# An S5 scan and a long convolution on one core: the written order of the steps replaced by another one

## The chip, the cores and the metric

The kernel runs on one core of a Trainium2 chip. The metric is the device time of one execution in microseconds (us). Traces are of one profiled execution each. Engines are called PE (TensorE), DVE (VectorE), ACT (ScalarE), POOL (GpSimd) and SP (SyncE, which here issues DMAs); PEld is PE's loading of weights.

## The reference

Two layers on sequences of 2048 steps and 640 channels, whose outputs are laid side by side. A is a diagonal complex state space model (640 states) with input and output projections; B multiplies a gated long convolution by q.

```python
def _A_ref(x, Lambda_re, Lambda_im, B_re, B_im, C_re, C_im, log_dt, Dskip):
    Lam_bar = jnp.exp(dt * Lam)
    B_bar = ((Lam_bar - 1.0) / Lam)[:, None] * Bmat
    Bu = jnp.einsum("bld,pd->blp", x + 0j, B_bar)
    for t in range(L):
        h = Lam_bar[None, :] * h + Bu[:, t, :]
    y = 2.0 * jnp.einsum("blp,dp->bld", hseq, Cmat).real + x * Dskip[None, None, :]

def _B_ref(q, k, v, shift_k, ssm_k, ssm_D):
    for t in range(ks):
        k_shift = k_shift + k_pad[:, t:t + S, :] * shift_k[:, ks - 1 - t][None, None, :]
    kv = k_shift * v
    ...
    y = y + kv * ssm_D[None, None, :]
    return q * y

return jnp.concatenate([a, b], axis=-1)
```

The line left out is a convolution of kv with ssm_k along the sequence, by FFT of length 4096.

## The kernel before

The work is cut into named items. `make_plan` gives each item an engine, the items that it needs and a function that records its instructions; `ORDER`, one long string, lists all items in the order in which they are recorded. Each engine carries out its own instructions strictly in that order, and SP likewise starts its DMAs in that order: an instruction that waits holds up everything behind it on its engine. Semaphores between engines follow from the data. The deps, costs and latencies in the plan don't act at run time; only `ORDER` does.

A name with `@0`, `@2`, `@4` or `@6` writes to one of four PSUM slots (`ps0` to `ps3`, two banks each). A slot can be written again when what was in it has been copied out. A name with `!` takes the item's other engine: an eviction (a copy from PSUM to SBUF) goes to DVE rather than ACT (`copy`, lines 467 and 469), and the swap of k's halves, `kS`, to ACT rather than DVE (`swap_k`, lines 625 and 627).

Layer A has five groups of 128 states, `j` = 0 to 4, and four sequence phases `s` (step mod 4). `v{s}_{j}` are the input matmuls (L522, L524, L525), `ve` their evictions; phase 0 is rotated (`rs`), scanned (`sc`, L551), turned back (`ra`, `rout`), and the other phases follow from it by `oa{s}_{j}` (L563 to L565) and `od{s}_{j}` (L570, L571), all on DVE. `p{i}_{s}` is the output projection for 128 rows of a phase (L584, with the skip term at L589): it needs all five groups of its phase. `yo` evicts it, `yd` stores it. The projection (3, 2) is done in two halves, `a` and `b`.

Layer B has five groups `G` of 128 channels. `kT`, `vT`, `hs`, `qi` load (the first two with a DMA transpose), `tap` is the short convolution on PE (L650), `kv` the product with v on DVE (L655), `kvo` and `kvs` store kv and load it back rearranged. Two matmul stages of a transform follow: `s1` (L666) and `s2` (L679), each with four parts for the filter (`h`) and for kv (`k`), each evicted (`s1he`, `s1ke`, `s2he`, `s2ke`). The product in frequency is `ya` (L691, L692) and `y` (L697) on DVE, in two halves. `inv` (L705 to L708) is four parts of the inverse, evicted by `zs`; `zt` transposes the result by DMA (L716); `fin` is the last matmul stage (L724), `ob` the product with q on DVE (L729), `od_G` the store. `y{G}_0` is needed by `inv{G}_0` and `inv{G}_1`, `y{G}_1` by the other two.

The first lines of `ORDER` prepare constants, tables and the first input matmuls. After them, items of layer A and layer B alternate.

Of the kernel before, what the change touches and what calls it, by code (L numbers as in the profile page):

```python
# [940 lines left out]

ORDER = """
lv1! pc lsk lv0! lv4 B0 pc2 dc dc3 wm0@0 lv2 zer lv3 pc3 dc2 wm1@2 B1 gp1 dsel x1 tsk@4 gp0 bt0@6 tske@4 dS0 tv@0 wm2@2 pp tve@0
bt1@4 x2 pk den exp wm3@2 be1@4 rho Fi wm4@0 rr be0!@6 v1_1@2 tp0 dD trig1 prr drhs G1 lam tp1 v1_0@4 x3 dL1 pow ve1_1@2 dL2 dL0
tab0 dcm@0 gam v2_1@6 gp3 aRM vT0 ve1_0!@4 tab1 tp2 dcol@0 dG B3 v2_0@2 G3 kT0 tp3 ve2_1!@6 tab2 dRM v3_1@4 ve2_0!@2 tab3 tp4 B4
x0 v3_0@0 tab4 ve3_1!@4 hp0 kS0 G0 hp1 bg1@6 ve3_0!@0 B2 H0 bg2@2 gp2 CT0 bge1!@6 tap0_0@4 H1 tap0_1@0 hp2 kv0_0@4 v0_0@6
kv0_1@0 bge2@2 hp3 H2 dS1 hs0 kvo0 bg3@4 H3 ve0_0!@6 kT1 v0_1@2 rs0 bge3@4 ca0 sc0 bg0@0 ve0_1@2 v1_3@6 bge0@0 rs1 G2 v1_2@4 sc1
ve1_3@6 CT1 v2_3@2 ve1_2@4 ra1 kS1! kvs0 had0 rout1 s1h0_2@0 vT1 nH ve2_3@2 s1h0_3@6 v2_2@4 oa2_1 s1he0_2@0 od2_1 s1he0_3@6
oa3_1 s1h0_0@2 od3_1 ve2_2@4 tap1_0@0 s1he0_0@2 s1h0_1@6 cs0 v3_2@4 s1he0_1@6 ra0 ca1 rout0 tap1_1@2 ve3_2@4 hs1 oa2_0 s1k0_1@6
v0_2@4 s1ke0_1@6 od2_0 kT2 kv1_0@0 kv1_1@2 s1k0_2@6 ve0_2@4 s1k0_3@0 cs1 s1k0_0@2 s1ke0_3@0 v3_3@4 s1ke0_0@2 qi0 kvo1 rs2  # L950
s1ke0_2@6 s2k0_3@0 dS2 ve3_3@4 s2h0_3@2 sc2 s2k0_1@6 s2ke0_3@0 v0_3@4 s2he0_3@2 s2ke0_1@6 had1 ra2 kS2! rout2 s2k0_2@0 vT2 oa2_2
v1_4@2 ve0_3@4 od2_2 s2ke0_2@0 kvs1 rs3 s2h0_1@6 ve1_4@2 s2h0_0@4 s2h0_2@0 s2he0_1@6 v2_4@2 s2he0_0@4 sc3 s2he0_2@0 ra3 s1h1_1@6
ve2_4@2 s1h1_0@4 tap2_1@0 rout3 s1he1_1@6 tap2_0@2 kv2_1@0 s1he1_0@4 s1h1_2@6 kT3 kv2_0@2 s1he1_2@6 s2k0_0@0 s1h1_3@4 s2ke0_0@0
s1k1_2@6 ya0_1 v3_4@2 s1ke1_2@6 kvo2 hs2 s1he1_3@4 dS3 y0_1 s2h1_3@0 ve3_4@2 s1k1_0@6 s1k1_3@4 ya0_0 s2he1_3@0 v0_4@2 kS3! y0_0
s1ke1_3@4 vT3 inv0_2@0 ve0_4!@2 s1ke1_0@6 inv0_1@4 rs4 zs0_2@0 s2h1_1@2 zs0_1@4 tap3_0@6 s2he1_1@2 s1k1_1@0 had2 sc4 inv0_0@4
kvs2 s1ke1_1@0 s2h1_0@2 zs0_0@4 inv0_3@0 kv3_0@6 s2he1_0@2 tap3_1@4 zs0_3@0 ra4 s2k1_2@2 kT4 s2k1_3@6 s2ke1_2@2 kv3_1@4 s2k1_0@0
s2ke1_3@6 s2h1_2@2 rout4 s1h2_1@4 s2ke1_0@0 kvo3 s2k1_1@6 oa2_3 zt0_0 s1he2_1@4 p0_0@0 od2_3 s2ke1_1@6 oa2_4 s2he1_2@2 od2_4
kS4! s1h2_3@4 s1k2_2@6 p1_0@2 oa1_1 od1_1 zt0_1 yo0_0@0 s1ke2_2@6 dS4 s1he2_3@4 ya1_1 s1k2_1@0 s1h2_0@6 yo1_0@2 yd0_0 p0_2@4 vT4
s1ke2_1@0 s1he2_0@6 y1_1 ya1_0 s1h2_2@2 yd1_0 yo0_2@4 s1k2_0@0 hs3 s1k2_3@6 s1he2_2@2 p1_2@4 s1ke2_0@0 kvs3 y1_0 s1ke2_3@6 yd0_2
oa1_3 s2h2_1@2 od1_3 yo1_2@4 s2h2_2@0 s2he2_1@2 yd1_2 fin0_1@6 oa1_0 inv1_0@4 s2he2_2@0 od1_0 s2h2_0@2 zs1_0@4 fin0_0@0  # L960
s2he2_0@2 inv1_1@4 ob0_1@6 inv1_2@2 zs1_1@4 oa3_2 inv1_3@6 zs1_2@2 ob0_0@0 s2k2_0@4 zs1_3@6 od3_2 s2k2_1@2 od_0 s2k2_3@0
s2ke2_0@4 zt1_0 s2k2_2@6 oa1_4 s2ke2_1@2 tap4_1@4 od1_4 s2ke2_2@6 s1k3_3@2 s1ke3_3@2 s2h2_3@6 kv4_1@4 s2ke2_3@0 s1k3_2@2 ya2_0
s1k3_0@4 s2he2_3@6 zt1_1 p2_2@0 s1ke3_2@2 s1ke3_0@4 had3 y2_0 qi1 s1h3_1@6 ya2_1 yo2_2@0 s1h3_0@2 tap4_0@4 s1he3_1@6 yd2_2
s1h3_2@0 s1he3_0@2 s1k3_1@6 kv4_0@4 s1ke3_1@6 inv2_0@2 s1he3_2@0 y2_1 fin1_0@6 kvo4 s1h3_3@4 zs2_0@2 inv2_1@0 hs4 oa3_3
s1he3_3@4 inv2_2@2 od3_3 zs2_1@0 s2h3_3@4 zs2_2@2 oa3_4 s2h3_1@0 s2he3_1@0 ob1_0@6 fin1_1@2 s2he3_3@4 s2k3_0@0 ob1_1@2 kvs4
inv2_3@6 s2ke3_0@0 od3_4 s2k3_1@4 zs2_3@6 od_1 s2k3_3@2 s2h3_0@0 s2ke3_1@4 oa1_2 zt2_0 p3_0@6 s2he3_0@0 od1_2 s2ke3_3@2 had4
ya3_0 s2h3_2@4 yo3_0@6 s2k3_2@0 s2he3_2@4 s1h4_0@2 s2ke3_2!@0 s1h4_3@6 s1he4_0@2 s1h4_2@4 y3_0 s1h4_1@0 s1he4_2@4 p2_0@2
s1he4_3@6 zt2_1 ya3_1 s1he4_1@0 s1k4_0@4 y3_1 yo2_0@2 s1k4_3@6 s2h4_0@0 s1ke4_0@4 s1k4_2@2 oa3_0 yd2_0 s1ke4_3@6 inv3_3@4 yd3_0
qi2 od3_0 s2he4_0@0 inv3_2@6 s1ke4_2@2 inv3_0@0 zs3_2!@6 zs3_3@4 inv3_1@2 zs3_0!@0 fin2_0@6 zs3_1@2 s1k4_1@4 s2h4_3@0 s1ke4_1@4
zt3_0 s2h4_2@2 s2he4_3!@0 s2he4_2@2 s2k4_3@4 s2k4_2@0 s2ke4_3@4 ob2_0@6 fin2_1@2 s2ke4_2@0 s2k4_0@4 zt3_1 ob2_1@2 s2k4_1@6  # L970
s2ke4_0@4 s2h4_1@0 ya4_1 p0_3@2 s2ke4_1@6 od_2 s2he4_1@0 y4_1 p0_1@4 yo0_3@2 ya4_0 yd0_3 y4_0 fin3_0@6 yo0_1@4 inv4_2@0 yd0_1
inv4_0@2 qi3 zs4_2@0 inv4_3@4 zs4_0@2 inv4_1@0 zs4_3@4 fin3_1@2 zs4_1!@0 p3_3@4 zt4_1 ob3_1@2 p2_3@0 zt4_0 ob3_0@6 p1_3@2 od_3
p1_1@6 yo1_3@2 yd1_3 p2_1@2 yo1_1@6 qi4 yd1_1 p3_1@6 yo2_1@2 yd2_1 yo2_3@0 yd2_3 fin4_1@2 yo3_1@6 fin4_0@0 ob4_1@2 yd3_1 p3_2a@6
p3_2b@2 yo3_3@4 ob4_0@0 yd3_3 od_4 yo3_2a@6 yo3_2b@2 yd3_2a yd3_2b
"""


# [66 lines left out]
```

## Time and profile before

| what | value |
|---|---|
| median of 3 runs | 201.82 us (201.66 to 201.91) |
| the profiled execution, whole time | 201.48 us |
| its span, first to last instruction | 199.7 us |
| PE busy | 185.5 us, 93% of the span |
| PEld busy | 128.0 us, 64% |
| DVE busy | 165.0 us, 83% |
| ACT busy | 153.9 us, 77% |
| POOL busy | 24.8 us, 12% |
| DMA | 32.61 MB, 163 GB/s in the mean |
| granted TensorE clock | 0.998 |

Busy time of an engine counts its instructions from start to end, once where they overlap. A PE instruction that waits in the middle of a group can look busy. The span leaves out what lies around the kernel's own instructions, 1.8 us here. Lines are those of the kernel printed above.

### The profile page before, as it was taken

The page shows a single profiled execution, that of the slowest core. Times are in us where ns is not written, and L with a number is a line of the kernel's source. Part 1 is how long each engine was busy: PE and PEld are TensorE (multiplying, and loading weights), DVE is VectorE, ACT ScalarE, POOL GpSimd, SP SyncE. Part 2 cuts the span into 40 slices and gives each one's busy share as a digit, 9 for nine tenths or more (in the row PEclk, how much of TensorE's full clock was granted, in tenths as well). Part 3 has the DMA queues.
Part 4 walks back from the last instruction along what each step waited for, and adds up shares of the span by engine and source line. Part 5 has one row for each costly group of instructions (what it writes and reads, how often), then busy time and mean ns, then how long its engine had stood idle before and what let it go on. Part 6 is the DMA issues. An engine that isn't in the chain of part 4 may idle for free. (4 is left out here: it accounts for less than half of the span.)

```text
span 199.7 us, 7507 instructions
## 1 busy us (share of the span) xinstructions
PE 185.5 (93%) x3328; PEld 128.0 (64%) x3340; DVE 165.0 (83%) x285; ACT 153.9 (77%) x190; POOL 24.8 (12%) x55
## 2 busy tenths in 40 slices
...
GB/s 129 201 216 220 207 235 221 187 207 110 82 159 186 147 67 27 241 163 83 213 193 176 154 173 132 155 256 136 203 151 147 147 170 150 129 153 198 147 126 138
DMA packets 125052, 32.61 MB, mean 163 GB/s; under 512 B 120919, under 2 KB 124380, under 8 KB 125020
## 3 DMA queue, kind: packets, MB, share of 16 engines
...
q10 hardware_dynamic: 40, 0.01, 0.0%
...
## 5 line engine op out<-in xcount | busy, mean ns | idle before, releaser
L522 PE MATMUL ps<-xT,BT 128*128 128x512 bf16 x188 | 47.6, 379 | 1.2 <-DMA xT<-in_A_x_dram 0.6
L584 PE MATMUL ps<-Cs,hs 128*128 128x320 bf16 x240 | 36.3, 299 | 0.3 <-ACT Xs L469 0.3
L469 ACT CAST BT<-ps 128x640 bf16<-128x640 f32 (+3 forms) x20 | 14.0, 703 | 25.1 <-PE ps L589 24.4
L522 PEld LDWEIGHTS <-BT 128*128 128x128 bf16 x200 | 18.6, 98 | 22.4 <-ACT BT L469 0.9
L584 PEld LDWEIGHTS <-hs 128*128 128x128 bf16 x240 | 21.9, 98 | 8.0 <-issue 0.2
L729 DVE TENSOR_TENSOR qb<-ps,qb 128x1024 bf16<-128x1024 f32 x10 | 12.0, 1219 | 15.8 <-PE ps L724 15.7
L679 PEld LDWEIGHTS <-G 128*64 128x64 bf16 x640 | 19.1, 110 | 5.3 <-issue 4.1
L469 ACT CAST As_kv<-ps 128x1024 bf16<-128x1024 f32 x20 | 20.0, 1041 | 0.3 <-PE ps L666 0.3
L469 ACT CAST As_h<-ps 128x1024 bf16<-128x1024 f32 x20 | 19.8, 1040 | 0.0
L469 ACT CAST Hf<-ps 128x1024 bf16<-128x1024 f32 x19 | 19.3, 1044 | 0.0
L469 ACT CAST zz<-ps 128x1024 bf16<-128x1024 f32 x17 | 17.2, 1034 | 2.3 <-PE ps L708 2.3
L469 ACT CAST Xs<-ps 128x1024 bf16<-128x1024 f32 x19 | 18.8, 1035 | 0.0
L707 PE MATMUL ps<-Xs,H 128*128 128x128 bf16 x80 | 17.5, 219 | 1.1 <-issue 1.1
L705 PE MATMUL ps<-Xs,H 128*128 128x128 bf16 x80 | 17.5, 219 | 0.9 <-ACT As_h L469 0.5
L706 PE MATMUL ps<-Xs,H 128*128 128x128 bf16 x80 | 17.5, 219 | 0.3 <-DVE Xs L697 0.3
L708 PE MATMUL ps<-Xs,H 128*128 128x128 bf16 x80 | 17.5, 219 | 0.0
L697 DVE TENSOR_TENSOR Xs<-Xs,rot 128x1024 bf16<-128x1024 bf16 x20 | 12.9, 686 | 0.2
L691 DVE TENSOR_TENSOR rot<-Xs,Hf 128x2048 bf16<-128x2048 bf16 x10 | 12.2, 1221 | 0.8 <-ACT BT L469 0.5
L692 DVE TENSOR_TENSOR Xs<-Xs,Hf 128x2048 bf16<-128x2048 bf16 x10 | 12.2, 1224 | 0.5
L679 PE MATMUL ps<-As_kv,G 128*64 128x128 bf16 x320 | 11.5, 220 | 1.0 <-DVE vT L655 0.5
L679 PE MATMUL ps<-As_h,G 128*64 128x128 bf16 x320 | 11.8, 221 | 0.7 <-ACT Xs L469 0.7
L655 DVE TENSOR_TENSOR vT<-ps,vT 128x1024 bf16<-128x1024 f32 x10 | 11.9, 1215 | 0.4 <-PE ps L650 0.4
...
## 6 DMA issues: line engine op xcount, KB each, us to landing
...
kv_rows<-vT SPq DMA_DIRECT2D x5, 512.0 KB, 5.1
...
qb<-in_B_q_dram SPq DMA_DIRECT2D x5, 512.0 KB, 4.2
out_dram<-qb SPq DMA_DIRECT2D x5, 512.0 KB, 5.1
...
```

Source lines behind the costliest of these rows:

```text
L469: self.nc.scalar.copy(out=out, in_=in_)
L522: mm(o, lhsT=self.BT[:, r, k, j * 128:(j + 1) * 128], rhs=xT[:, k, :], start=(k == 0), stop=(s == 1 and k == NT - 1))
L584: mm(o[:, 0:320], lhsT=h[:, r, ts], rhs=self.Cs[:, r, j, c0:c0 + 320], start=(j == 0 and r == 0), stop=(not on_pe and j == NT - 1 and r == 1))
L679: self.nc.tensor.matmul(o[64 * e:64 * e + 64, c:c + 128], lhsT=self.G[:, r, k, :], rhs=As[:, k, :], start=True, stop=True)
L691: tt(out=self.cross(), in0=X[:, ::-1, :], in1=self.Hf[:, 1:2, hs].to_broadcast([128, 2, 1024]), op=ALU.mult)
L692: tt(out=X, in0=X, in1=self.Hf[:, 0:1, hs].to_broadcast([128, 2, 1024]), op=ALU.mult)
L697: self.nc.vector.tensor_tensor(out=X[:, r, :], in0=X[:, r, :], in1=cr[:, r, :], op=ALU.add if r else ALU.subtract)
L705: mm(o_re, lhsT=self.H[:, 0, k1, :], rhs=yre, start=True, stop=False)
L706: mm(o_re, lhsT=self.H[:, 2, k1, :], rhs=yim, start=False, stop=True)
L707: mm(o_im, lhsT=self.H[:, 1, k1, :], rhs=yre, start=True, stop=False)
L708: mm(o_im, lhsT=self.H[:, 0, k1, :], rhs=yim, start=False, stop=True)
L729: self.nc.vector.tensor_tensor(out=self.qb[:, :, cs].rearrange("p a (i c) -> p a i c", c=4), in0=ps[:].rearrange("p a n -> p (a n)").rearr ...
```

## The change

Nothing but the string `ORDER` differs. It holds the same items. The first line of items stays word for word and the next ones keep their items and order and only take other PSUM slots; from the scans of the groups 0 and 1 on (`sc0`) the order is another. The marks `!` differ too: before, `ve0_4`, `s2ke3_2`, `zs3_2`, `zs3_0`, `s2he4_3`, `zs4_1` are evicted by DVE and `kS1` to `kS4` copied by ACT in that part; now `zs2_1`, `zs4_1`, `zs4_3` and `kS4`. The first changed lines and the last ones:

```diff
@@ -941,37 +941,37 @@
...
-kv0_1@0 bge2@2 hp3 H2 dS1 hs0 kvo0 bg3@4 H3 ve0_0!@6 kT1 v0_1@2 rs0 bge3@4 ca0 sc0 bg0@0 ve0_1@2 v1_3@6 bge0@0 rs1 G2 v1_2@4 sc1
-ve1_3@6 CT1 v2_3@2 ve1_2@4 ra1 kS1! kvs0 had0 rout1 s1h0_2@0 vT1 nH ve2_3@2 s1h0_3@6 v2_2@4 oa2_1 s1he0_2@0 od2_1 s1he0_3@6
...
+kv0_1@4 bge2@0 hp3 H2 dS1 hs0 kvo0 bg3@2 H3 ve0_0!@6 kT1 v0_1@0 rs0 bge3@2 ca0 sc0 bg0@4 ve0_1@0 v1_3@6 bge0@4 had0 s1h0_1@2 CT1
+G2 s1h0_2@0 rs1 sc1 kS1 ra0 nH rout0 cs0 vT1 s1he0_1@2 s1he0_2@0 ve1_3@6 v1_4@4 s1h0_3@2 s1h0_0@0 v2_3@6 kvs0 hs1 s1he0_0@0
...
+od_0 inv1_0@2 zs1_0@2 inv1_1@0 zs1_1@0 zt1_0 zt1_1 s2k2_3@4 s2h2_3@6 s2h2_1@2 s2k2_1@0 s2ke2_3@4 s2he2_3@6 s2he2_1@2 s2h2_0@4
+s2ke2_1@0 s2he2_0@4 tap4_0@6 s2k2_0@2 s2ke2_0@2 kv4_0@6 s1h3_2@0 tap4_1@4 s1he3_2@0 kv4_1@4 rout4 s1h3_0@2 s1k3_1@6 s1he3_0@2
...
+s1k4_0@6 s1k4_1@2 s1ke4_0@6 s1ke4_1@2 fin2_1@4 inv3_0@0 zs3_0@0 inv3_3@6 zs3_3@6 oa1_2 ob2_1@4 fin2_0@2 inv3_2@0 ob2_0@2
...
+zt3_1 yd1_2 qi3 s2he4_1@0 s2ke4_2@2 s2ke4_1@6 ya4_1 y4_1 p0_1@0 yo1_1@4 yo0_1@0 fin3_0@2 p0_3@6 fin3_1@4 yo0_3@6 inv4_2@0 ya4_0
+y4_0 ob3_0@2 ob3_1@4 yd0_1 yd3_2a yd0_3 od_3 yd1_1 inv4_1@6 inv4_3@2 inv4_0@4 zs4_2@0 zs4_0@4 zs4_1!@6 zs4_3!@2 zt4_0 zt4_1 qi4
+p3_0@0 p1_3@6 p2_1@2 p3_1@4 yo2_1@2 yo1_3@6 yo3_0@0 fin4_0@2 p2_3@6 yo2_3@6 fin4_1@0 yd2_2 yd1_3 yd2_1 yd2_3 yd3_0 yo3_1@4 yd3_1
...
```

Three places as the built programs have them. First, ACT and DVE just after the first scans. `ps` is a PSUM slot, `kS` the swapped k, `As_h` what `s1he` writes, `hs` what `ve` writes. ACT before:

```order
L469 CAST hs_146<-ps_67 128x1024
L469 CAST hs_144<-ps_66 128x1024
L625 COPY kS<-kT 64x1032 x2
L469 CAST hs_146<-ps_65 128x1024
L469 CAST As_h<-ps_64 128x2x32x16
L469 CAST As_h<-ps_67 128x2x32x16
```

and DVE now, from the scan of group 1 (L551) on:

```order
L536 TENSOR_TENSOR rot<-tabs,z_151 128x1024
L537 TENSOR_TENSOR rot<-tabs,z_151 128x1024
L541 TENSOR_TENSOR rot<-rot 128x512 x2
L551 SCALAR_TENSOR_TENSOR z_151<-rr_88,rot 128x512 x2
L627 COPY kS<-kT 64x1032 x2
L536 TENSOR_TENSOR rot<-tabs,z_150 128x1024
L537 TENSOR_TENSOR rot<-tabs,z_150 128x1024
```

The copies of `kS1` stood on ACT behind two evictions of `v`; they now stand on DVE behind the second scan.

Second, DVE around `ob2_1` and `ob2_0` (the two rows of L729). Before:

```order
L467 CAST zz<-ps_67 128x8x32x4
L467 CAST zz<-ps_64 128x8x32x4
L467 CAST Hf<-ps_64 128x2x512
L729 TENSOR_TENSOR qb<-ps_67,qb 128x16x64
L729 TENSOR_TENSOR qb<-ps_65,qb 128x16x64
L691 TENSOR_TENSOR rot<-Xs,Hf 128x2048
L692 TENSOR_TENSOR Xs<-Xs,Hf 128x2048
L697 TENSOR_TENSOR Xs<-Xs,rot 128x1024 x2
```

Now:

```order
L563 TENSOR_SCALAR rot<-hs_144,lam 128x1024
L564 TENSOR_SCALAR rot<-hs_144,lam 128x512
L565 TENSOR_SCALAR rot<-hs_144,lam 128x512
L729 TENSOR_TENSOR qb<-ps_66,qb 128x16x64
L729 TENSOR_TENSOR qb<-ps_65,qb 128x16x64
L570 TENSOR_TENSOR rot<-rot,hs_144 128x1024
L571 TENSOR_TENSOR hs_144<-rot 128x1024
L563 TENSOR_SCALAR rot<-hs_142,lam 128x1024
```

Before, three evictions by DVE stand ahead of the pair and the product `ya4_1` behind it. Now the pair stands between `oa1_2` and `od1_2`, and the order inside it is `ob2_1` first; four more pairs of `oa` and `od` follow before `ya4_1`.

Third, the end of SP's queue. `qb` holds q and then the output of layer B, `BT` the outputs of layer A, `zz` both sides of `zt`. Before:

```order
L716 DMA_TRANSPOSE zz<-zz 128x16x128 x2
L734 DMA out_dram<-qb 128x16x128
L611 DMA out_dram<-BT 128x640
L719 DMA qb<-in_B_q_dram 128x16x128
L611 DMA out_dram<-BT 128x640 x5
L734 DMA out_dram<-qb 128x16x128
L611 DMA out_dram<-BT 128x320 x2
```

Now:

```order
L734 DMA out_dram<-qb 128x16x128
L611 DMA out_dram<-BT 128x640
L716 DMA_TRANSPOSE zz<-zz 128x16x128 x2
L719 DMA qb<-in_B_q_dram 128x16x128
L611 DMA out_dram<-BT 128x640 x6
L734 DMA out_dram<-qb 128x16x128
L611 DMA out_dram<-BT 128x640
L611 DMA out_dram<-BT 128x320
```

The store of group 3 (`od_3`) stood behind the last transposes and stands ahead of them now; behind the last store of layer B (`od_4`) there were the two halves of the last projection, and there are now a whole one and one half.

More of the change, by code (lines that the diff above doesn't have):

```diff
@@ L943 @@
 lv1! pc lsk lv0! lv4 B0 pc2 dc dc3 wm0@0 lv2 zer lv3 pc3 dc2 wm1@2 B1 gp1 dsel x1 tsk@4 gp0 bt0@6 tske@4 dS0 tv@0 wm2@2 pp tve@0
-bt1@4 x2 pk den exp wm3@2 be1@4 rho Fi wm4@0 rr be0!@6 v1_1@2 tp0 dD trig1 prr drhs G1 lam tp1 v1_0@4 x3 dL1 pow ve1_1@2 dL2 dL0
-tab0 dcm@0 gam v2_1@6 gp3 aRM vT0 ve1_0!@4 tab1 tp2 dcol@0 dG B3 v2_0@2 G3 kT0 tp3 ve2_1!@6 tab2 dRM v3_1@4 ve2_0!@2 tab3 tp4 B4
-x0 v3_0@0 tab4 ve3_1!@4 hp0 kS0 G0 hp1 bg1@6 ve3_0!@0 B2 H0 bg2@2 gp2 CT0 bge1!@6 tap0_0@4 H1 tap0_1@0 hp2 kv0_0@4 v0_0@6
@@ L947 @@
-kv0_1@0 bge2@2 hp3 H2 dS1 hs0 kvo0 bg3@4 H3 ve0_0!@6 kT1 v0_1@2 rs0 bge3@4 ca0 sc0 bg0@0 ve0_1@2 v1_3@6 bge0@0 rs1 G2 v1_2@4 sc1
-ve1_3@6 CT1 v2_3@2 ve1_2@4 ra1 kS1! kvs0 had0 rout1 s1h0_2@0 vT1 nH ve2_3@2 s1h0_3@6 v2_2@4 oa2_1 s1he0_2@0 od2_1 s1he0_3@6
-oa3_1 s1h0_0@2 od3_1 ve2_2@4 tap1_0@0 s1he0_0@2 s1h0_1@6 cs0 v3_2@4 s1he0_1@6 ra0 ca1 rout0 tap1_1@2 ve3_2@4 hs1 oa2_0 s1k0_1@6
-v0_2@4 s1ke0_1@6 od2_0 kT2 kv1_0@0 kv1_1@2 s1k0_2@6 ve0_2@4 s1k0_3@0 cs1 s1k0_0@2 s1ke0_3@0 v3_3@4 s1ke0_0@2 qi0 kvo1 rs2
@@ L951 @@
[L951 to L971, printed above, removed]
@@ L972 @@
-inv4_0@2 qi3 zs4_2@0 inv4_3@4 zs4_0@2 inv4_1@0 zs4_3@4 fin3_1@2 zs4_1!@0 p3_3@4 zt4_1 ob3_1@2 p2_3@0 zt4_0 ob3_0@6 p1_3@2 od_3
-p1_1@6 yo1_3@2 yd1_3 p2_1@2 yo1_1@6 qi4 yd1_1 p3_1@6 yo2_1@2 yd2_1 yo2_3@0 yd2_3 fin4_1@2 yo3_1@6 fin4_0@0 ob4_1@2 yd3_1 p3_2a@6
-p3_2b@2 yo3_3@4 ob4_0@0 yd3_3 od_4 yo3_2a@6 yo3_2b@2 yd3_2a yd3_2b
+bt1@4 x2 pk den exp wm3@0 be1@4 rho Fi wm4@2 rr be0!@6 v1_1@0 tp0 dD trig1 prr drhs G1 lam tp1 v1_0@2 x3 dL1 pow ve1_1@0 dL2 dL0
+tab0 dcm@4 gam v2_1@6 gp3 aRM vT0 ve1_0!@2 tab1 tp2 dcol@4 dG B3 v2_0@0 G3 kT0 tp3 ve2_1!@6 tab2 dRM v3_1@2 ve2_0!@0 tab3 tp4 B4
```

21 lines of the change are left out of this document (added).

## The prediction

> **What bounds the kernel now.** I read the views in this order: the busy time by stage, the chain that ended last, VectorE's (DVE's) timeline ahead of that chain, and the end of the DMA queue. The stages first (columns: stretch in us, its length, busy us of each engine):
>
> ```profile
> 34.80:169.70 134.90, 128.46 (x2843) 91.79 (x2851) 130.55 (x198) 118.25 (x132) 0.00 (x0) 1.00 0.81 156
> 169.70:194.90 25.20, 25.17 (x277) 19.66 (x276) 5.86 (x5) 7.14 (x10) 0.00 (x0) 1.00 0.72 150
> 194.90:199.70 4.80, 0.01 (x1) 0.00 (x0) 0.00 (x0) 0.42 (x1) 0.00 (x0) 0.91 0.59 143
> ```
>
> From the first scans (34.8) to 169.7 the fullest engine is DVE, 130.55 of 134.90 us; TensorE (PE) has 128.46. From 169.7 on DVE has almost nothing and PE is full. The last 4.8 us hold only an eviction and stores. The chain of waits says what happens at 169.7:
>
> ```profile
> 169.68 0.04 issue
> 169.73 0.22 PE ps L706
> ...
> 172.51 0.47 PE ps L724 x16
> 172.98 1.36 PE ps L584 x10
> 174.34 0.14 PE ps L589 x3
> ...
> 194.76 0.15 PE ps L589 x3
> 194.92 0.02 issue
> 194.94 0.42 ACT BT L469
> ```
>
> It begins at 169.7, when DVE has finished y4_0 and the inverse matmuls (L705 to L708) can go on; from there it is PE without a gap to 194.92. So the time is a sum of three: DVE until y4_0 (169.7), the PE work that is left then (25.2), and the closing stores (4.8).
>
> DVE ahead of that point:
>
> ```profile
> 154.68 2.36 DVE L467 CAST zz<-ps 128x1024 bf16<-128x1024 f32 x2
> 157.87 1.23 DVE L467 CAST Hf<-ps 128x1024 bf16<-128x1024 f32 x1 [0.84 <-PE ps L679]
> 159.01 1.21 DVE L729 TENSOR_TENSOR qb<-ps,qb 128x1024 bf16<-128x1024 f32 x1
> 160.47 1.23 DVE L729 TENSOR_TENSOR qb<-ps,qb 128x1024 bf16<-128x1024 f32 x1 [0.24 <-PE ps L724]
> 161.61 1.22 DVE L691 TENSOR_TENSOR rot<-Xs,Hf 128x2048 bf16<-128x2048 bf16 x1
> ```
>
> DVE waits for PE only for 0.84 and 0.24 us here: PE is barely ahead of it, so neither engine can be relieved alone for long.
>
> **The change, part by part.** All PE work is the same. Four things differ.
>
> (a) *DVE's load ahead of y4_0.* Five evictions that DVE had (ve0_4, s2ke3_2, zs3_2, zs3_0, s2he4_3) go to ScalarE (ACT), one (zs2_1) comes to DVE, and kS1, kS2 and kS3 come from ACT to DVE.
>
> ```profile
> L627 DVE COPY kS<-kT 64x1032 bf16<-64x1032 bf16 x2 | 0.9, 436 | 0.1
> L625 ACT COPY kS<-kT 64x1032 bf16<-64x1032 bf16 x8 | 8.4, 1050 | 0.2
> L469 ACT CAST Hf<-ps 128x1024 bf16<-128x1024 f32 x19 | 19.3, 1044 | 0.0
> ```
>
> An eviction on DVE costs 2.36 / 2 = 1.18, a kS two copies of 436 ns, 0.87. DVE: -5 x 1.18 + 1.18 + 3 x 0.87 = -2.1 us. ACT: +4 x 1.04 - 3 x 2 x 1.05 = -2.1 us, so ACT, at 118 of 134.9, covers what it takes over. If ACT could not, at most the four evictions, 4.2 us, would come back. Taken: -2.1.
>
> (b) *What is left for PE after y4_0.* Before: three inverse matmul groups (169.73 to 172.51, 2.78), fin3_1 (0.47), seven projections (2 x (1.36 + 0.14) = 3.0 each, counting the two halves as one) and fin4 (2 x 0.47): 25.2. Now p1_1 and the first half p3_2a, and fin3_1, stand ahead of it, p3_0 behind it: 6.5 projections are left, so 2.78 + 19.5 + 0.94 = 23.2. But inv4_3 and inv4_0 use the PSUM slots of fin3_0 and fin3_1, which ob3_0 and ob3_1 empty only after y4_0: 2 x 1.18 until inv4_0 may start, against 1.86 of PE work by then, and with the hand-over 0.7 lost. Net -1.3; bounds -2.0 (no loss) and 0. The work moved forward needs room: 1.5 + 0.5 more PE work in 2.1 us less is 4.1, and PE is idle 134.90 - 128.46 = 6.4 in that stretch. It fits, not by much. The Trainium skill's "Perfetto Trace Analysis", section "Identifying the Most-Contended Engine", holds that matmul busy time misjudges how near PE is to its limit and that weight-load busy time should be used; by that (91.79 of 134.90) the room would be far larger. In the tail, where PE is full, weight loads read 19.66 of 25.20, so here their full mark is nearer to 78% than to 100%, which the page does not say. The sum is the same by either reading; by the skill's, the second rival below would be less likely than I put it.
>
> Behind the inverse groups fin4 waits for the transposes of zz. Now four projections (12 us) stand between; the pair took 5.75 to issue and about 5 to land after each issue:
>
> ```profile
> 173.97 5.75 SPq L716 DMA_TRANSPOSE zz<-zz  x2
> zz<-zz SPq DMA_TRANSPOSE x10, 4.9
> ```
>
> The second issues about 2.9 after the first, so some 7.8 us after the last eviction, 1.2 to 2.4 us after inv4_0. It stays covered; uncovered it would cost what exceeds 12.
>
> (c) *The end.* Before, the 512 KB store od_4 is issued at 193.91, hardly before PE ends:
>
> ```profile
> 193.91 0.38 SPq L734 DMA_DIRECT2D out_dram<-qb  x1
> 194.38 2.25 SPq L611 DMA_DIRECT2D out_dram<-BT  x2
> out_dram<-qb SPq DMA_DIRECT2D x5, 512.0 KB, 5.1
> out_dram<-BT SPq DMA_DIRECT2D x2, 80.0 KB, 2.9
> SPq L1039 <- DMA out_dram<-qb: 1.2, 1, 1.2
> ```
>
> 193.91 + 5.1 = 199.0, and the closing wait names it. Now p3_3 and p3_2b (4.5 us of PE) stand behind fin4_1, so od_4 goes out about 3.2 us before PE ends and lands 1.9 after it. Next late is the last half: 0.7 for eviction and issue, 2.9 to land, 0.7 to close as now, 4.3 in place of 4.8. Taken: -0.5; bounds 0 and -1.0.
>
> (d) *The wait at ob2_1.* Ahead of fin2_1 PE now has 12 fewer items: p2_2, p3_0, four inverse groups, fin2_0 and five s2 groups.
>
> ```profile
> 157.19 1.08 PE L679 MATMUL ps<-As_h,G 128*64 128x128 bf16 x32
> 141.21 0.49 DVE L563 TENSOR_SCALAR rot<-hs,lam 128x1024 bf16<-128x1024 bf16 x1
> 142.14 0.68 DVE L570 TENSOR_TENSOR rot<-rot,hs 128x1024 bf16<-128x1024 bf16 x1
> 143.46 0.30 DVE L634 TENSOR_TENSOR h_st<-h_st,dcol_b 128x32 bf16<-128x32 bf16 x1
> ```
>
> PE: 2 x 3.0 + 4 x 0.93 + 0.47 + 5 x 0.54 = 12.9. Ahead of ob2_1 DVE has fewer by the 2.1 of (a), four oa/od pairs (143.46 - 141.21 = 2.25 each), od1_2 (1.32) and ob2_0 (1.2): 13.6. So DVE is there 0.7 earlier relative to PE than before, when it waited 0.24: a wait of 0.9. Then ob2_0 needs fin2_0, which PE has two inverse groups later (2 x 0.93 + 0.47 = 2.3) while ob2_1 fills 1.2: 1.1 more. Behind them on DVE stand od1_2, four pairs, ya4 and y4, for which PE's last inverse groups wait; od_2 waits too. So 2.0 if PE loses as much on its way as before. PE's losses stand here:
>
> ```profile
> 100.00:120.00 20.00, 19.87 (x474) 16.15 (x473) 19.62 (x34) 18.00 (x21) 0.00 (x0) 1.00 0.98 171
> 120.00:140.00 20.00, 16.58 (x525) 14.03 (x521) 19.53 (x30) 18.31 (x21) 0.00 (x0) 1.00 0.87 170
> ```
>
> Of 6.4 us, 3.4 are lost in 120 to 140, where PE runs 18 short items (s1, s2, tap, inv, fin), one projection, and 18 more, each handing one of four PSUM slots through an eviction of 1.04. Up to fin2_1 the old order has runs of 15, 18 and 18 and most of a fourth, the new one of 17 and 14; elsewhere long groups stand between. So PE may come earlier by 0 to 3.4; I take 0.8, a quarter, since those losses are partly waits for DVE. Wait: +1.2, bounds 0 and 2.0 plus any new PE loss.
>
> (e) *Moves that I cost at nothing.* On SP the pair zt0 now stands ahead of kvo3 and kT4 instead of behind them:
>
> ```profile
> 97.95 6.69 SPq L716 DMA_TRANSPOSE zz<-zz  x2
> kT<-in_B_k_dram SPq DMA_TRANSPOSE x5, 4.3
> ```
>
> kT4 then lands 6.69 + 0.5 + 4.3 = 11.5 us after zs0_3 at the earliest. Its reader, kS4 on ACT, stands 20 evictions behind zs0_3, at about 0.98 each 19.6: covered by 8 us. kS1, kS2, kS3 on DVE stand behind scans or y0; were one load late, all of DVE would wait. The early kv1 pair has the least cover: I see no price for it in these rows and leave it in the upper bound.
>
> **The sum.** The profiled execution took 201.48 (its span 199.7 and 1.8 around it); the median of the runs is 201.82, 0.34 more. 201.48 - 2.1 - 1.3 - 0.5 + 1.2 = 198.8; with the 0.34, 199.1.
>
> **The rivals.**
> *1. No new wait.* PE gains enough from its shorter runs that ob2 finds its matmuls done: 201.82 - 2.1 - 1.3 - 0.5 = 197.9. For it: the shorter runs. Against: in the old order DVE already waited at this very place.
> *2. PE's slots bind (slower).* In the run of 17 short items from fin0_1 to s1k3_0 PE waits for slots as in 120 to 140, and the work moved ahead of y4_0 finds no room. DVE already waits at ob2_1, so every further us that PE loses ahead of it counts whole; the gain is gone from 2.7 us. One more stretch like that row costs 3.4: 202.5; two, 205.9. For it: the 3.4 in that row, DVE's waits of 0.84 and 0.24. Against: fewer such runs than before.
> *3. The two sides cancel.* PE loses about 2.7, or the tail of (b) gains nothing and ob2 waits the full 2.0 and 0.6 more: 201.8, no change. The change would then only move waits about.
>
> **How the numbers follow.** Forecast 0.50 (own range 198.2 to 201.2), rival 1 0.15, rival 2 0.29, rival 3 0.06. A measurement of this kernel tells about 0.2% from no change. Faster 0.50 - 0.01 + 0.15 = 0.64; same 0.06 + 0.01 = 0.07; slower 0.29. Low end: rival 1 and another 1 us of DVE's 4.35 idle regained, 196.9. High end: rival 2 with its one stretch and 0.5 more, 203.0, which leaves out its two-stretch form.
>
> **What would show it.** (a): eight DVE copies at L627, two at L625, and fewer L467 casts on DVE. (b): the chain from y4_0 to PE's end 23 to 24 us. (c): the 512 KB store 3 us before PE ends, 4.3 behind PE's end. (d): ob2_1 or ob2_0 with a wait of 1 to 2 us on PE L724, y4_0 done near 168.8. The forecast is wrong if DVE waits for PE, ACT or a load by more than 4 us in sum, or if PE's idle time ahead of y4_0 exceeds 6.4.

## The result, and the profile after

The changed kernel takes 198.56 us in the median of four runs (198.43 to 199.01); the kernel before, run beside it, 201.74 in the median of four. The ratio is 0.985, with a 95% interval of 0.9825 to 0.9879: 1.5% faster, 0.5 us from the forecast of 199.1. Its profiled execution took 199.01 us with a span of 197.2, against 201.48 and 199.7: 2.5 us less in both. Of the experiments' runs below, one of new_mix was slow (202.10 us at a lower granted clock, 0.991) and isn't in its ratio.

The stages of the changed kernel, cut where its own y4_0 ends and where PE ends, and the two stretches that rival 2 spoke of (columns as in the prediction):

```profile
34.80:169.50 134.70, 129.77 (x2861) 91.59 (x2860) 129.88 (x201) 115.50 (x130) 0.00 (x0) 1.00 0.83 158
169.50:193.80 24.30, 24.27 (x275) 19.15 (x271) 6.98 (x7) 6.43 (x9) 0.00 (x0) 1.00 0.72 157
193.80:197.20 3.40, 0.00 (x0) 0.00 (x0) 0.00 (x0) 0.43 (x1) 0.00 (x0) 1.00 0.41 116
100.00:120.00 20.00, 17.46 (x423) 13.27 (x420) 19.41 (x26) 19.57 (x21) 0.00 (x0) 1.00 1.00 180
120.00:140.00 20.00, 19.42 (x517) 16.27 (x515) 19.24 (x32) 17.63 (x20) 0.00 (x0) 1.00 0.89 151
149.00:169.50 20.50, 20.44 (x309) 16.36 (x306) 19.70 (x33) 12.92 (x17) 0.00 (x0) 1.00 0.62 125
```

The first three rows are the three terms of the prediction's sum. From 149 on PE has no idle time left (20.44 of 20.50, then 24.27 of 24.30). The chain of waits, which before began at y4_0, now runs on PE through that moment without a break:

```profile
169.31 0.47 PE ps L724 x16
169.78 0.06 PE ps L705
...
193.63 0.16 PE ps L589 x3
193.81 0.43 ACT BT L469
```

y4_0 ends at 168.21 + 1.29 = 169.50 (DVE's row below), while PE is still at fin3_1 and then at inv4_2, which doesn't need it: y4_0 is no longer on the chain. DVE's timeline at the two places that the prediction named:

```profile
147.43 0.49 DVE L563 TENSOR_SCALAR rot<-hs,lam 128x1024 bf16<-128x1024 bf16 x1
147.84 0.35 DVE L564 TENSOR_SCALAR rot<-hs,lam 128x512 bf16<-128x512 bf16 x1
148.10 0.35 DVE L565 TENSOR_SCALAR rot<-hs,lam 128x512 bf16<-128x512 bf16 x1
148.36 2.35 DVE L729 TENSOR_TENSOR qb<-ps,qb 128x1024 bf16<-128x1024 f32 x2
...
166.95 1.23 DVE L692 TENSOR_TENSOR Xs<-Xs,Hf 128x2048 bf16<-128x2048 bf16 x1
168.21 1.29 DVE L697 TENSOR_TENSOR Xs<-Xs,rot 128x1024 bf16<-128x1024 bf16 x2
```

The row of L729 (ob2_1 and ob2_0) has no bracket: no wait there. The rows also show how DVE's instructions stand to each other, which matters below: L564, which doesn't read what L563 wrote, starts 0.08 before L563 ends, while L697 starts 0.03 after L692, whose result it reads.

The end of SP's queue in the changed kernel, its issues:

```profile
190.97 0.39 SPq L734 DMA_DIRECT2D out_dram<-qb  x1
193.03 1.57 SPq L611 DMA_DIRECT2D out_dram<-BT  x2
```

the time from issue to landing of the half stores of layer A (two such stores; the figure is that of the last one):

```profile
out_dram<-BT SPq DMA_DIRECT2D x2, 80.0 KB, 1.6
```

and what the closing instruction waits for:

```profile
SPq L1039 <- DMA out_dram<-BT: 0.8, 2, 0.4
SPq L1039 <- DMA out_dram<-qb: 0.4, 1, 0.4
```

The 512 KB store od_4 goes out 2.8 us before PE ends, and the last half store lands in 1.6 us instead of 2.9.

| step (us) | before | now | difference | forecast |
|---|---|---|---|---|
| y4_0 ends | 169.67 | 169.50 | -0.2 | -0.9 (a: -2.1, d: +1.2) |
| from there to the last eviction | 25.27 | 24.31 | -1.0 | -1.3 (b) |
| from there to the end of the span | 4.76 | 3.39 | -1.4 | -0.5 (c) |
| span | 199.7 | 197.2 | -2.5 | -2.7 |

The last eviction starts at 194.94 before and at 193.81 now. The sum was right to 0.2; its terms were not. The experiments ask why.

### The profile page after: what moved, and what is told of

Same layout as the page of the kernel before. It is cut to its first block, busy times and chain, and to the rows that moved or that the text cites. A ratio compares the mean times of both kernels' runs of the same rounds, so it can differ in the third digit from the quotient of the medians.

```text
span 197.2 us, 7514 instructions
## 1 busy us (share of the span) xinstructions
PE 185.9 (94%) x3340; PEld 127.3 (65%) x3340; DVE 165.5 (84%) x288; ACT 150.5 (76%) x187; POOL 24.8 (13%) x55
## 4 chain that ended last, share of the span: by engine, by line
PE 72%; ACT 16%; DVE 8%; issue 2%; POOL 0%; POOLq 0%; DVEq 0%; ACTq 0%
PE ps L584 23%; PE ps L522 16%; PE ps L679 7%; PE ps L666 4%; PE ps L650 4%; ACT zz L469 3%; ACT Xs L469 3%; PE ps L524 2%; PE ps L525 2%; PE ps L589 2%; ACT As_kv L469 2%; ACT Hf L469 2%; PE ps L705 2%; DVE H L388 2%; PE ps L724 1%
## 5 line engine op out<-in xcount | busy, mean ns | idle before, releaser
L522 PE MATMUL ps<-xT,BT 128*128 128x512 bf16 x200 | 48.9, 379 | 1.5 <-DMA xT<-in_A_x_dram 0.7
L729 DVE TENSOR_TENSOR qb<-ps,qb 128x1024 bf16<-128x1024 f32 x10 | 11.9, 1219 | 14.5 <-PE ps L724 14.1
L469 ACT CAST Hf<-ps 128x1024 bf16<-128x1024 f32 x20 | 20.3, 1038 | 0.5 <-PE ps L679 0.4
L469 ACT CAST Xs<-ps 128x1024 bf16<-128x1024 f32 x20 | 20.2, 1031 | 0.2
L697 DVE TENSOR_TENSOR Xs<-Xs,rot 128x1024 bf16<-128x1024 bf16 x20 | 12.9, 687 | 0.3
L691 DVE TENSOR_TENSOR rot<-Xs,Hf 128x2048 bf16<-128x2048 bf16 x10 | 12.3, 1225 | 1.0 <-ACT Xs L469 0.3
L655 DVE TENSOR_TENSOR vT<-ps,vT 128x1024 bf16<-128x1024 f32 x10 | 11.9, 1220 | 1.1 <-PE ps L650 0.8
L692 DVE TENSOR_TENSOR Xs<-Xs,Hf 128x2048 bf16<-128x2048 bf16 x10 | 12.2, 1225 | 0.7
L584 PE MATMUL ps<-Cs,h 128*128 128x320 bf16 x80 | 12.1, 299 | 0.0
L679 PE MATMUL ps<-As_kv,G 128*64 128x128 bf16 x320 | 11.9, 221 | 0.2 <-ACT As_h L469 0.2
```

What stands on the lines that cost most here:

```text
L469: self.nc.scalar.copy(out=out, in_=in_)
L522: mm(o, lhsT=self.BT[:, r, k, j * 128:(j + 1) * 128], rhs=xT[:, k, :], start=(k == 0), stop=(s == 1 and k == NT - 1))
L584: mm(o[:, 0:320], lhsT=h[:, r, ts], rhs=self.Cs[:, r, j, c0:c0 + 320], start=(j == 0 and r == 0), stop=(not on_pe and j == NT - 1 and r == 1))
L655: self.nc.vector.tensor_tensor(out=self.vT[:, ts], in0=ps[:].rearrange("p a n -> p (a n)"), in1=self.vT[:, ts], op=ALU.mult)
L679: self.nc.tensor.matmul(o[64 * e:64 * e + 64, c:c + 128], lhsT=self.G[:, r, k, :], rhs=As[:, k, :], start=True, stop=True)
L691: tt(out=self.cross(), in0=X[:, ::-1, :], in1=self.Hf[:, 1:2, hs].to_broadcast([128, 2, 1024]), op=ALU.mult)
```

## The experiments

Two theories stand against each other throughout. The *DVE theory* is the prediction's: the sum of DVE's load from the scans to y4_0 sets when y4_0 is done. The *slot theory*: PE and ACT, handing four PSUM slots to each other, set the time, and DVE waits or not as they let it. All kernels compute the whole reference; only `ORDER` differs. Ratios are to the kernel before, run beside each; "last" is the start of the last eviction, "closing" what follows it.

| kernel | ratio (95%) | y4_0 | last | closing |
|---|---|---|---|---|
| before | 1 | 169.67 | 194.94 | 4.76 |
| changed | 0.985 (0.9825 to 0.9879) | 169.50 | 193.81 | 3.39 |
| old_a | 1.0181 (1.0153 to 1.021) | 173.93 | 199.38 | 4.72 |
| old_kS | 1.0132 (1.0111 to 1.0152) | 172.78 | 198.05 | 4.75 |
| old_ev3 | 1.008 (1.0065 to 1.0096) | 171.17 | 196.63 | 4.77 |
| new_kS_act | 1.0201 (1.0144 to 1.0258) | 177.62 | 202.23 | 3.37 |
| new_kS4_dve | 0.9895 (0.9866 to 0.9924) | 169.53 | 193.85 | 3.45 |
| new_kS4_zs | 0.9936 (0.9914 to 0.9958) | 171.43 | 195.63 | 3.37 |
| new_p11_late | 0.9971 (0.9946 to 0.9996) | 169.95 | 196.79 | 3.41 |
| new_c_back | 0.9909 (0.9883 to 0.9935) | 169.14 | 193.46 | 4.64 |
| old_c | 0.9983 (0.9958 to 1.0008) | 169.87 | 196.26 | 3.44 |
| old_c2 | 0.9942 (0.9919 to 0.9965) | 170.17 | 195.43 | 3.37 |
| new_mix | 0.9866 (0.9845 to 0.9887) | 169.53 | 193.85 | 3.45 |
| new_again | 0.9849 (0.983 to 0.9868) | 169.55 | 193.88 | 3.42 |

**The new load in the old order.** old_a makes the exchange of (a) in the order of before (without zs2_1):

```diff
-ve0_4!@2 s2ke3_2!@0 zs3_2!@6 zs3_0!@0 s2he4_3!@0 kS1! kS2! kS3!
+ve0_4@2 s2ke3_2@0 zs3_2@6 zs3_0@0 s2he4_3@0 kS1 kS2 kS3
```

> The old order with term (a) alone: five evictions go from DVE to ACT, kS1 to kS3 from ACT to DVE; DVE's load ahead of y4_0 falls by 5 x 1.18 - 3 x 0.87 = 3.3 us. DVE theory (DVE sets y4_0, 2.1 of load are 2.1 of time): y4_0 2 to 3 us earlier and the time 2 us shorter, near 199.7. Slot theory (PE and ACT, through the four PSUM slots, are as near to being the limit as DVE): PE still reaches the last inverse groups near 169, DVE waits instead, and the time changes by less than 0.7.

Measured: 1.8% slower, so both theories missed. Two parts of the exchange were then run by themselves. old_kS moves only the copies:

```diff
-kS1! kS2! kS3!
+kS1 kS2 kS3
```

> The order of before; only kS1, kS2 and kS3 go from ACT to DVE (ACT -6.3 us, DVE +2.6). DVE theory (the sum of DVE's load ahead of y4_0 sets y4_0): y4_0 and the time 2 to 2.6 us later, 204. Slot theory (PE and ACT through four PSUM slots set the time, DVE has slack here and there): DVE +2.6 is met by evictions that come 2.1 us earlier per kS, so the time is between 201 and 203 and DVE's waits for PE and ACT shrink by 1 us or more.

1.3% slower, 2.7 us; y4_0 comes 3.1 later. Two stretches of its profile (columns as above):

```profile
60.00:80.00 20.00, 18.15 (x328) 10.36 (x324) 19.56 (x33) 16.28 (x18) 0.00 (x0) 1.00 0.48 105
120.00:140.00 20.00, 16.79 (x517) 14.19 (x515) 19.65 (x32) 17.85 (x20) 0.00 (x0) 1.00 0.81 172
```

The first of them in the kernel before; the second stands in the prediction:

```profile
60.00:80.00 20.00, 19.38 (x389) 11.38 (x378) 19.62 (x32) 18.47 (x20) 0.00 (x0) 1.00 0.48 107
```

ACT falls from 18.47 to 16.28 of 20 and DVE stays at 19.6: in the old order DVE is full up to about 140, so 2.7 us of copies there cost 2.7 us and a freer ACT brings nothing. The DVE theory is right here.

old_ev3 moves only three evictions, late in the program:

```diff
-zs3_2!@6 zs3_0!@0 s2he4_3!@0
+zs3_2@6 zs3_0@0 s2he4_3@0
```

> The order of before; only zs3_2, zs3_0 and s2he4_3 go from DVE to ACT (DVE -3.5 us, ACT +3.1, all between 145 and 160 us). DVE theory: y4_0 3.5 us earlier, time 198 to 199. Slot theory: ACT's evictions there stand back to back, PE's slots come free later, DVE waits at ob2_0, ob2_1 or the zz evictions for 4 us or more in sum, time 202 to 205.

0.8% slower, with 3.5 us less on DVE. Its timelines of DVE, at ob2_0 and ob2_1, and of ACT, at the four `zs3`:

```profile
157.68 1.23 DVE L729 TENSOR_TENSOR qb<-ps,qb 128x1024 bf16<-128x1024 f32 x1 [3.19 <-DMA qb<-in_B_q_dram]
162.32 1.23 DVE L729 TENSOR_TENSOR qb<-ps,qb 128x1024 bf16<-128x1024 f32 x1 [3.41 <-PE ps L724]
...
154.96 3.82 ACT L469 CAST zz<-ps 128x1024 bf16<-128x1024 f32 x4
158.57 1.12 ACT L469 CAST As_kv<-ps 128x1024 bf16<-128x1024 f32 x1
```

and ACT at the same place in the kernel before, where DVE took the other two:

```profile
155.16 1.07 ACT L469 CAST zz<-ps 128x1024 bf16<-128x1024 f32 x1
156.45 1.01 ACT L469 CAST zz<-ps 128x1024 bf16<-128x1024 f32 x1 [0.23 <-PE ps L708]
157.36 1.02 ACT L469 CAST As_kv<-ps 128x1024 bf16<-128x1024 f32 x1
```

ACT's next eviction comes 1.2 us later (158.57, not 157.36), PE gets its slots later, and DVE, which arrives early, waits 6.6 us: first for the load of q for group 2, which before had landed when DVE came at 159.01, then for PE. The slot theory is right here. The two parts make 2.7 + 1.6 = 4.3 us, old_a 3.7; its other two evictions, ve0_4 and s2ke3_2, were not run alone. So neither engine sets the whole stretch: DVE does until about 140, PE with ACT after it, and the exchange adds to DVE in the one part and relieves it in the other. A sum over the whole stretch gives it the wrong sign.

**The same copies in the new order.** new_kS_act returns them to ACT:

```diff
-kS1 kS2 kS3
+kS1! kS2! kS3!
```

> The new order with kS1, kS2 and kS3 back on ACT: DVE's load falls by 2.6 us, ACT's rises by 6.3. DVE theory: y4_0 2 us earlier, the time the same or up to 1 shorter. Slot theory: PE waits for evictions, the time 2 to 4 us longer (200.5 to 202.5).

2.0% slower than before, about 7 us slower than the changed kernel: the slot theory's direction, but more than its 2 to 4 us. DVE's waits (us in total, times, longest), of which the changed kernel has 0.8 of the first and none of the second:

```profile
DVE vT L655 <- PE ps L650: 6.6, 4, 3.4
DVE rot L536 <- ACT z L469: 5.1, 1, 5.1
```

and ACT's timeline at kS3:

```profile
74.95 2.12 ACT L625 COPY kS<-kT 64x1032 bf16<-64x1032 bf16 x2 [1.69 <-DMA kT<-in_B_k_dram]
```

Three copies of 2.12 and ACT's wait of 1.69 for k are 8.1; y4_0 moves by 177.62 - 169.50 = 8.1. The two agree, which fits an early part that ACT sets, though the sum alone doesn't prove it. That the new order needs these copies on DVE, the run shows.

new_kS4_dve goes on in that direction with kS4:

```diff
-zs1_2@2 kS4! v0_4@4 fin0_1@6
+zs1_2@2 v0_4@4 fin0_1@6
...
-ve0_4@4 rs4 dS4 had3
+ve0_4@4 rs4 kS4 dS4 had3
```

new_kS4_zs has that edit and also gives zs2_1 to ACT:

```diff
-zs2_1!@0
+zs2_1@0
```

> The new order with the last kS on DVE too. In the changed kernel's chain of waits the two copies of kS4 on ACT stand at 103.7 to 105.8, with evictions before and after them. Slot theory: ACT's 2.1 us leave that chain, PE loses 1 to 2 us less in 100 to 120, DVE has 0.9 more to do and uses up its lead of 0.9 at y4_0: the time 0.3 to 0.9 shorter. DVE theory: the time 0.9 longer.

> As the one before, and zs2_1 is evicted by ACT in place of DVE, so DVE's load is 0.3 below the changed kernel's and ACT's 1.1 below. Slot theory: the time 0.5 to 1.5 shorter than the changed kernel's. DVE theory: 0.3 shorter.

new_kS4_dve has the changed kernel's profile to 0.1 us in every step, though DVE has 0.9 us more to do: neither theory's figure. By the ratios it is 0.4% slower than the changed kernel, 0.9 us, which the DVE theory gives; the profiled execution doesn't show it, the intervals overlap, and I leave it open. new_kS4_zs missed both forecasts: it is 1.7 us slower than the changed kernel by the ratios, and y4_0 comes 1.9 later than in new_kS4_dve, from which only zs2_1 differs. With that eviction on ACT, DVE waits at ob1_0.

```profile
127.89 2.36 DVE L729 TENSOR_TENSOR qb<-ps,qb 128x1024 bf16<-128x1024 f32 x2 [2.41 <-ACT Hf L469]
```

**The projection moved ahead.** new_p11_late puts p1_1 behind the inverse groups again:

```diff
-od_2 oa3_4 od3_4 p1_1@4 zt3_0
+od_2 oa3_4 od3_4 zt3_0
...
-p3_0@0 p1_3@6 p2_1@2 p3_1@4
+p1_1@0 p1_3@6 p2_1@2 p3_1@4 yo1_1@0 yd1_1 p3_0@0
```

> The new order with term (b) partly undone: the projection p1_1 stands behind the last inverse groups instead of ahead of them. PE then reaches the first of them 3.0 us earlier (166.4) and must wait for y4_0 (169.5). Slot theory, with DVE 0.9 us ahead at that place: the time 3.0 - 0.9 = 2.1 longer, near 200.7, and PE idle for about 2 us just ahead of y4_0. DVE theory with nothing to gain from PE's order: the time 3.0 longer.

2.4 us slower than the changed kernel by the ratios, 3.0 by the spans of the two profiles (200.2 and 197.2), so it doesn't tell the theories apart; it does show (b). PE now waits for y4, which it did not in the changed kernel:

```profile
169.41 0.23 PE L705 MATMUL ps<-Xs,H 128*128 128x128 bf16 x1 [0.55 <-DVE Xs L697]
170.01 0.22 PE L706 MATMUL ps<-Xs,H 128*128 128x128 bf16 x1 [0.37 <-DVE Xs L697]
```

So most of the projection's 3.0 us, 2.4 or more, had found room ahead of y4_0.

**The closing.** new_c_back keeps the changed order up to the inverse groups and ends as before, with the pair fin4_0 and fin4_1 ahead of a single projection:

```diff
-fin4_0@2 p2_3@6 yo2_3@6 fin4_1@0 ... ob4_0@2 ob4_1@0 od_4 p3_3@2 yo3_3@2 yd3_3 p3_2b@6 yo3_2b@6 yd3_2b
+p2_3@6 ... p3_2b@2 ... fin4_0@0 fin4_1@4 ... yo3_2b@2 ... yd3_2b p3_3@6 ob4_0@0 ob4_1@4 od_4 yo3_3@6 yd3_3
```

old_c does the reverse in the order of before:

```diff
-p3_1@6 yo2_1@2 yd2_1 yo2_3@0 yd2_3 fin4_1@2 yo3_1@6 fin4_0@0
+yo2_3@0 yd2_3 fin4_1@6 fin4_0@0 ob4_1@6 yo2_1@2 yd2_1 p3_1@2
```

> The new order with term (c) undone: fin4_0 and fin4_1 stand together ahead of one last whole projection (3.0 us), so od_4 is issued about 1.0 before PE ends, as in the old order. Theory: PE's end unchanged, the closing stretch 4.8 in place of 3.4, the time 1.4 longer (200.0). Rival (the closing was short for another reason, such as less other traffic): less than 0.5 longer.

> The old order with term (c) alone: the two last matmul stages of layer B (fin4) stand ahead of the last whole projection of phase 1 and both halves, so the store od_4 is issued about 3.6 us before PE ends in place of 1.0. Both theories: PE's end unchanged (195), the stretch from PE's end to the end of the span 3.4 to 3.9 in place of 4.8, the time 0.9 to 1.4 shorter. Rival for the changed kernel's 3.4 us closing: it is the luck of one execution or of a smaller last store; then no change here.

new_c_back closes in 4.64 and is 1.2 us slower than the changed kernel by the ratios. old_c closes in 3.44, yet gains only 0.2%, which its interval doesn't tell from nothing: PE ends 1.3 later. Its timeline of PE at fin4_0, then of ACT:

```profile
189.47 0.63 PE L724 MATMUL ps<-Mq,zz 128*128 128x64 bf16 x16 [0.83 <-ACT BT L469]
...
194.21 1.62 ACT L469 CAST BT<-ps 128x640 bf16<-128x640 f32 x3 [4.19 <-DMA out_dram<-BT]
```

fin4_0 waits until an output's eviction has cleared its slot, and ACT until a store has cleared an output buffer.

That was my edit and not the closing, so old_c2 orders the projections such that no slot is waited for:

```diff
-p3_3@4 ... p2_3@0 ... p1_3@2 ... p1_1@6 ... p2_1@2 ... p3_1@6 ... fin4_1@2 yo3_1@6 fin4_0@0
+p1_1@4 ... p2_3@0 ... p1_3@2 ... p2_1@6 ... p3_3@4 ... fin4_1@2 fin4_0@0 ob4_1@2 p3_1@6
```

> The order of before up to the inverse groups; after them fin4_1 and fin4_0 ahead of p3_1 and both halves of p3_2, as in old_c, but with the projections in another order and other slots, so that fin4_0 finds its slot empty and no output buffer is waited for. Theory that the closing is a term of its own: PE ends as before (194.9, within 0.3), od_4 is issued near 191, the closing is 3.5 instead of 4.8, the time 200.5, 0.994 of before. Rival, that the moved store only makes something else late (an output store, the last eviction): PE or the closing gives it back, ratio 0.998 or more as in old_c.

0.9942, with the forecast time of 200.5 against 200.62 measured. y4_0 came 0.5 later in its profiled execution, PE's end with it, and the closing is 3.37. Its last half store lands in 1.6 us too.

In all fourteen profiles the closing is either 4.6 to 4.8 or 3.4 to 3.5; before, the 512 KB store goes out 1.0 us ahead of the last eviction (193.91 and 194.94), in the changed kernel 2.8. Why the step is 1.4 and not 0.5 stands in the durations of the issues of layer A's last stores (minimum, median, maximum in ns). Before:

```profile
L611 SPq DMA_DIRECT2D out_dram<-BT x3: 332/1006/1193, 192.3 to 195.4; - x3
```

now:

```profile
L611 SPq DMA_DIRECT2D out_dram<-BT x2: 332/332/333, 193.0 to 194.3; - x2
```

Right behind the 512 KB store the two small ones took 1.0 and 1.2 us to issue, and the last of them 2.9 to land; in the changed kernel the last took 0.33 and 1.6. The slow issue isn't needed for the late landing, as the end of new_c_back shows:

```profile
192.44 0.38 SPq L734 DMA_DIRECT2D out_dram<-qb  x1
194.18 0.33 SPq L611 DMA_DIRECT2D out_dram<-BT  x1
SPq L1040 <- DMA out_dram<-qb: 1.8, 1, 1.8
```

Its last store (160 KB) is issued 1.7 us behind the 512 KB store and in 0.33 us, yet takes 2.6 to land (the wait for qb ends at 194.51 + 1.8 = 196.3, the landing is at 196.8): like the half store of before (2.9), it lands about 0.5 us after the 512 KB store. So a 512 KB store that is issued early doesn't only land early itself, the last store no longer lands behind it.

**DVE's neighbours.** In the changed order `y` mostly follows straight on its `ya`. new_mix moves three other items of DVE in between (dS4 from its place behind rs4; new_again is the changed kernel, on the same chip):

```diff
-ya0_1 y0_1 ya0_0 y0_0 kS3 dS3 ... ya1_1 y1_1
+ya0_1 dS3 y0_1 ya0_0 kS3 y0_0 ... ya1_1 dS4 y1_1
```

> The changed order; three scalings on DVE (dS3, kS3, dS4) put between a ya and its y, so that y no longer follows at once on the ya it reads. Gap theory (a DVE instruction that reads what the one before it wrote starts about 0.1 us later than an independent one): the three pairs take 0.1 us less each, 0.3 in sum. DVE theory: the time is 0.3 us shorter than the changed kernel's, 0.9835 of before. Slot theory (PE sets the end from 149 us on): no difference, within 0.2 us.

> The changed kernel unaltered, for a comparison on the same chip: 0.985 of before by every theory.

DVE's timeline in new_again, then in new_mix:

```profile
67.83 1.23 DVE L692 TENSOR_TENSOR Xs<-Xs,Hf 128x2048 bf16<-128x2048 bf16 x1
69.08 1.29 DVE L697 TENSOR_TENSOR Xs<-Xs,rot 128x1024 bf16<-128x1024 bf16 x2
```

```profile
67.82 1.23 DVE L692 TENSOR_TENSOR Xs<-Xs,Hf 128x2048 bf16<-128x2048 bf16 x1
68.96 0.69 DVE L638 TENSOR_TENSOR diagS<-id,sk_b 128x512 bf16<-128x512 bf16 x1
69.56 1.29 DVE L697 TENSOR_TENSOR Xs<-Xs,rot 128x1024 bf16<-128x1024 bf16 x2
...
76.25 0.69 DVE L536 TENSOR_TENSOR rot<-tabs,z 128x1024 bf16<-128x1024 bf16 x1 [0.53 <-ACT z L469]
```

With dS3 between, both neighbours start 0.09 before the end of the one ahead; without it L697 starts 0.02 after. (With kS3 between there was no overlap, so that place gained nothing.) What DVE saved it waited away, 0.53 of it at rs3 for ACT; y4_0 is the same as new_again's, and the time too within its interval. The gap theory holds for the instructions, the slot theory for the time.

No version here beats the changed kernel.

## Why the prediction was right, and where it was not

The forecast time and its direction were right, and the sum of the terms too. But the terms were off by +0.7, +0.3 and -0.9, which nearly cancel; the agreement to 0.5 us is partly luck.

**(a) and (d), y4_0: -0.9 forecast, -0.2 measured**, which two single profiles don't tell from no move. DVE's load fell as worked out: the durations of its instructions from the end of sc0 to y4_0, added up, are 136.92 us in 191 rows before and 134.79 in 193 now, -2.13 against -2.1. The step that failed is that a fall in that sum moves y4_0 by the same. Between the rows lies the rest: before, 128 of them start before the one ahead ends and save 10.93 us, small gaps take 2.71, waits of 0.15 us or more 1.53; now 110 overlap and save 9.50, gaps take 3.53, waits 1.22. 136.92 - 10.93 + 2.71 + 1.53 = 130.23, and 134.79 - 9.50 + 3.53 + 1.22 = 130.04. So 2.25 us came back as lost overlaps and gaps, which I had not counted. 18 pairs more have a gap: nine lie beside the copies of kS that came to DVE, and three are a `y` straight behind its `ya`. My price of 0.87 for a kS left that out:

```profile
41.57 2.33 DVE L551 TENSOR_TENSOR_SCAN z<-rr,rot 128x512 bf16<-128x512 f32 x2
43.94 0.88 DVE L627 COPY kS<-kT 64x1032 bf16<-64x1032 bf16 x2
44.85 0.69 DVE L536 TENSOR_TENSOR rot<-tabs,z 128x1024 bf16<-128x1024 bf16 x1
```

The wait (d), +1.2, did not come. fin2_1 on PE's timeline, before and in the changed kernel:

```profile
159.72 0.64 PE L724 MATMUL ps<-Mq,zz 128*128 128x64 bf16 x16
146.19 0.64 PE L724 MATMUL ps<-Mq,zz 128*128 128x64 bf16 x16
```

It is done 13.5 us earlier (160.36 and 146.83), where I had 12.9 and 0.8. But DVE comes to ob2_1 only 11.9 earlier (160.47 - 0.24 = 160.23 and 148.36), where I had 13.6: 1.5 us behind PE, so it didn't wait. All this is an account of where the time lies and not yet a cause. Against new_again, new_kS4_dve has 0.8 us more of instructions on DVE and new_mix 0.7 less of lost overlaps and gaps; in both y4_0 stayed at 169.53, because DVE's waits fell by 0.4 (and overlaps grew by 0.3) in the one and grew by 0.7 in the other. So in the new order neither DVE's load nor its gaps alone set y4_0, and which hand-over between PE, ACT and DVE does stays open. old_a showed besides that the exchange alone, in the old order, costs 3.7 us.

**(b), PE's work behind y4_0: -1.3 forecast, -1.0 measured.** The work moved ahead found its room (new_p11_late: 2.4 us by the ratios and 3.0 of span hang on p1_1). The loss of 0.7 at the slots of inv4_3 and inv4_0 did not occur; instead PE reaches the inverse groups after y4_0, not with it: the rest of fin3_1 (169.78 - 169.50 = 0.3) and inv4_2 (0.9) were still to do then, and 23.2 + 1.2 = 24.4 are the 24.3 measured. What was wrong is the frame: y4_0 doesn't begin the chain any more, PE's own idle time ahead of 149 does. From 34.8 to PE's end it is idle for 160.1 - 153.63 = 6.5 us before (128.46 + 25.17 busy) and for 159.0 - 154.04 = 5.0 now (129.77 + 24.27). Of these 1.5 us the last eviction gained 1.1; the other 0.4 is busy time of the same work, in a trace with 16 more matmul records (3136, not 3120), since some are missing in each. Which move in the order freed the idle time, no run isolates.

**(c), the closing: -0.5 forecast, -1.4 measured.** That the place of the 512 KB store sets the closing was right: new_c_back and old_c2 show it as a term by itself, worth 1.2 us in either order, give or take about 0.5 by their intervals. The sum behind it was not. I had od_4 land at 199.0, with 5.1 us, the middle value of five such stores. But SP's last issue before ends at 194.38 + 2.25 = 196.63, and the wait for qb behind it lasts 1.2, so od_4 landed at 197.8, after 3.9; the half stores came after it, the last at 195.4 + 2.9 = 198.3:

```profile
SPq L1039 <- DMA out_dram<-BT: 0.5, 2, 0.3
```

From there to the end of the span it is 1.4 us, not 0.7. In the terms of the forecast, 0.7 + 2.9 + 0.7, the changed kernel has 0.45 + 1.6 + 1.34 = 3.4. The term that was mis-sized is the landing of the last half store: I took its 2.9 as its own, and it was the 512 KB store's ahead of it. The Trainium skill's "DMA: Bandwidth & Descriptors", section "Two DMAs through the same engine are not ordered", says that within one queue of one DMA engine the descriptors start in order; the 2.9 and 1.6 fit that.

**(e), the moves costed at nothing**, held in the changed kernel, but barely: a kS on DVE waited 0.6 us for its load of k in new_c_back and 1.1 in new_p11_late, whose orders are the same up to there.

**The rivals.** Rival 1's condition came true (no wait at ob2), its time of 197.9 did not: y4_0 did not come earlier. Rival 2's place was real: in 100 to 120 PE lost 2.5 us (17.46 of 20). But 120 to 140, which had lost 3.4, now loses 0.6, so the losses changed places and did not add up. The weight-load reading of the Trainium skill's "Perfetto Trace Analysis", section "Identifying the Most-Contended Engine", would have made PE look 20% free in 149 to 169.5 (16.36 of 20.50), where PE is without a gap and sets the end.

**The marks.** DVE has the eight copies at L627 and ACT two at L625. PE's end came 24.3 us after y4_0 (23 to 24 forecast), od_4 went out 2.8 us before it (3), the closing took 3.4 (4.3), y4_0 ended at 169.5 (168.8), no wait stood at ob2 (1 to 2). Neither sign of a wrong forecast appeared: DVE's waits add up to 1.2 us (more than 4), and PE's idle time from 34.8 to y4_0 is 134.70 - 129.77 = 4.9 (more than 6.4).
